# Loading batch 1's keys and queries right behind batch 0's, ahead of all weights, into a buffer of the MLP's activations

## The chip, the cores and the metric

The kernel runs on one core of a Trainium2 chip. The metric is device time in microseconds (us), the median of several executions; lower is better. A profile is one execution; its span is some 2 us shorter than the time of the same execution. The granted clock is the share of TensorE's full clock that the profile records as allowed, 1.0 or 0.5 here. A load is issued when its engine starts it, and lands when its last data are in place.

## The reference

Two layers: attention over blocks that a Sinkhorn-normalized matrix mixes, then a Fourier mix and an MLP. Cut to what matters:

```python
B, H, S, D = 4, 8, 768, 64          # batch, heads, sequence, head size
P = sinkhorn(sort_net)              # 5 rounds, [B, H, 8, 8]
k_sorted = einsum('bhij,bhjcd->bhicd', P, k_blocks)   # 8 blocks of 96 rows
v_sorted = einsum('bhij,bhjcd->bhicd', P, v_blocks)
attn = softmax(q_blocks @ k_sorted.T / 8) @ v_sorted  # within each block
x = attn.reshape(B, S, 512)
u = x + real(fft(fft(x, axis=1), axis=2))
out = u + relu(layernorm(u) @ w_ch1) @ w_ch2          # 512 -> 2048 -> 512
```

## The kernel before

Five engines work from one static program: TensorE (PE), VectorE (DVE), ScalarE (ACT), GpSimd (POOL) and SyncE (SP). The order on each engine is fixed when the kernel is built. GpSimd issues the loads that convert float32 to float16: k, q, v and the two weights. They share one queue, q0. SyncE issues the loads of constant tables, on another queue, q1.

K and q of a batch come in two halves of four heads. Each half has a tile of its own, from a pool of two buffers per name:

```python
    def load_qk(b, hf):
        for src, nm in ((k, "k"), (q, "q")):
            t = wt([128, 4, 6, D], F16, nm + "16", 2)      # two buffers
            start(nc.gpsimd.dma_start(t..., src[b, 4 * hf:4 * hf + 4, :, :]...))
            qk[nm, b, hf] = t

    load_qk(0, 0)
    # ... (cut)
    vst = wt([128, BLK, D], F16, "hr", 2, "vst")            # v of batches 0 and 1
    for g in range(2):
        start(nc.gpsimd.dma_start(vst[:, 48 * g:48 * g + 48, :], ...))
    load_qk(0, 1)
    # ... memsets; the Sinkhorn rounds, ph[9] is their last step (cut)
    # SyncE's tables: eb, vsf, tab, dtab, cs, and
    lt2 = const.tile([97, 2, S], F16, name="lt2")
    start(nc.sync.dma_start(lt2, cn["lt"].ap()))            # 97 rows
    # ...
    for c in range(4):
        w = nc.gpsimd.dma_start(w1sb[:, c, :], w1v[:, c, :])
        gated(w, ph[9]) if c == 0 else start(w)             # w1, after Sinkhorn
    # ... scores of batch 0 (cut)
    load_qk(1, 0)                                           # batch 1, first half
    # ... v_mix(0, n): the mixed v of batches 0 and 1 (cut)
    for c in range(2):
        start(nc.gpsimd.dma_start(w2sb[:, 4 * c:4 * c + 4, :], ...))
    load_qk(1, 1)                                           # batch 1, second half
    for c in range(2, 4):
        start(nc.gpsimd.dma_start(w2sb[:, 4 * c:4 * c + 4, :], ...))
    # v1_gen, later: load_v(1), v of batches 2 and 3, into vcx in two loads
```

The copy `q_copy(b, hp)` puts q in the order in which PE transposes it. It runs on VectorE (L281). VectorE also turns probabilities into the operand of the product with v (L421), and that product is PE's L444. In `mlp`, each group takes a tile of the pool "hr", which has two buffers. The tile `vst` takes the first one at the start; the second is unused until the MLP's second group.

The softmax here doesn't subtract the row's maximum and nothing guards it: scores larger than these inputs give would overflow.

Of the kernel before, what the change touches and what calls it, by code (L numbers as in the profile page):

```python
# [10 lines left out]
F16 = mybir.dt.float16  # L11
# [9 lines left out]
D = 64  # L21
# [79 lines left out]
def kernel(  # L101
# [10 lines left out]
    nc = tc.nc  # L112
# [19 lines left out]
    def wt(shape, dtype, tag, bufs, nm=None):  # L132
        cnt[0] += 1
        return work.tile(shape, dtype, tag=tag, bufs=bufs,
                         name=f"{nm or tag}{cnt[0]}")
# [36 lines left out]
    def start(ins):  # L172
        return tc.keep_in_program_order(ins)
# [5 lines left out]
    def traced():  # L179
        return list(nc.cur_bb.bb.instructions)  # L180
# [8 lines left out]
    qk = {}  # L189

    def load_qk(b, hf):
        for src, nm in ((k, "k"), (q, "q")):
            t = wt([128, 4, 6, D], F16, nm + "16", 2)
            start(nc.gpsimd.dma_start(
                t.rearrange("p h r d -> p h (r d)"),
                src[b, 4 * hf:4 * hf + 4, :, :].rearrange(
                    "h (p r) d -> p h (r d)", r=6)))
            qk[nm, b, hf] = t

    load_qk(0, 0)  # L200
    pack = const.tile([128, 240], F32, name="pack")
    start(nc.sync.dma_start(pack, cn["pack"].ap()))
# [34 lines left out]
    for n in range(NKS):  # L237
        t = const.tile([128, NB, 128], F16, name=f"ksb{n}")
# [12 lines left out]
    mone = const.tile([128, 3], F32, name="mone")  # L251
    start(nc.gpsimd.memset(mone, 1.0))
    start(nc.gpsimd.tensor_tensor(mone, mone, mhalf, op=ALU.pow))

    sec0 = len(traced())
    rmax = const.tile([32, NB], F32, name="rmax")
# [43 lines left out]
    w2sb = const.tile([128, 16, DM], F16, name="w2sb")  # L300
    w1v = moe_w_ch1.rearrange("(c p) f -> p c f", p=128)
    w2v = moe_w_ch2.rearrange("(c p) m -> p c m", p=128)
# [48 lines left out]
    t = wt([128, H, NB, 16], F16, "bdk", 2)  # L351
# [564 lines left out]
    def sc(kk):  # L916
        es = new_es()
        t0 = scores(*kk[:2], 0, es)
        t1 = scores(*kk[:2], 1, es)
        return kk + (es, [max(a, c) for a, c in zip(t0, t1)])  # L920
# [11 lines left out]
    nc.scalar.copy(tkh, psk)  # L932
    vb_make(0, psm)
    k0[1] = sc(k0[1])
    load_qk(1, 0)
    for n in range(16):
        v_mix(0, n)
    last = {}
    for ins in traced()[sec0:]:
        if ins.engine in (EN.DVE, EN.Activation, EN.PE):  # L940
            if ins.engine in last:
                dep(ins, last[ins.engine])
            last[ins.engine] = ins
    for c in range(2):
        start(nc.gpsimd.dma_start(w2sb[:, 4 * c:4 * c + 4, :],
                                  w2v[:, 4 * c:4 * c + 4, :]))
    load_qk(1, 1)
    for c in range(2, 4):
        start(nc.gpsimd.dma_start(w2sb[:, 4 * c:4 * c + 4, :],
                                  w2v[:, 4 * c:4 * c + 4, :]))  # L950
    add(0, fft_gen())
# [47 lines left out]
```

## Time and profile before

| | before |
|---|---|
| time, median of 3 | 323.6 us (322.8 to 323.98) |
| span of the profiled execution | 321.6 us |
| PE busy | 290.4 us, 90% |
| PE busy from 40 to 50, from 50 to 60 us | 6.06, 4.80 of 10 us |
| granted TensorE clock | 0.5 from 22.5 to 29.3 and from 49.8 to 63.4 us |

From the page of the kernel before, its second part: the span in 40 slices of 8 us, the busy share in tenths, and the granted clock.

```profile
PE   0389974699899999999999999999999999999995
...
PEclk9986995599999999999999999999999999999999
```

After the ninth slice (about 72 us) PE is nearly full to the end. What can be won is in the first slices. The seventh one and its neighbours show a dip, and the clock drops behind it. The table of stretches of the kernel before (us; busy time and count of each engine; granted clock; share of the DMA engines; GB/s) says the same:

```profile
40.00:50.00 10.00, 6.06 (x112) 4.83 (x111) 6.45 (x17) 6.85 (x15) 4.08 (x5) 0.99 0.86 140
50.00:60.00 10.00, 4.80 (x48) 3.62 (x48) 8.45 (x18) 1.17 (x3) 1.14 (x1) 0.50 1.40 201
```

The waits of PE in the kernel before (who waited for whom: us in total, times, longest):

```profile
PE pf L444 <- DVE eb L421: 4.5, 1, 4.5
PE pf L666 <- DVE ee L641: 3.6, 1, 3.6
```

PE waits for VectorE's L421. VectorE's own timeline tells why L421 is late (start, duration, what; in brackets the idle time before it and what ended it):

```profile
45.90 1.01 DVE L456 TENSOR_TENSOR r<-pf,rz 128x384 f16<-128x384 f32 x2
50.87 0.36 DVE L281 COPY qr<-q 128x768 f16<-128x768 f16 x1 [3.96 <-DMA q<-in_q_dram]
51.15 1.28 DVE L421 TENSOR_SCALAR eb<-ex 96x384 f16<-96x384 f32 x2
```

L421 has its inputs since 47 us, but stands behind the copy of batch 1's q. The copy waits for a load. The chain of waits of the kernel before, in order of time (start, duration, what), goes through that load:

```profile
21.34 0.74 POOL k L194
22.08 28.77 DMA q<-in_q_dram
50.85 0.02 issue
50.87 0.36 DVE qr L281
51.23 0.28 DVE eb L421
51.51 0.05 issue
51.56 1.15 PE pf L444 x12
```

So a load of 384 KB took 28.77 us from issue to landing. A chain says what came last, not what it would have cost to come earlier: of the 28.77 us, 3.96 show as a wait.

### The profile page before, as it was taken

To read this page: it belongs to the slowest core of one execution; us is meant where nothing else is said; L and a number is where in the kernel's file an instruction comes from. 1 tells how busy PE (TensorE), PEld (TensorE's weight loads), DVE (VectorE), ACT (ScalarE), POOL (GpSimd) and SP (SyncE) were. 2 spreads that over 40 slices of the span, in tenths; PEclk is the share of its full clock that TensorE was granted. 3 is DMA by queue.
4 is the path that set the end of the run, shared out by engine and by line. 5 is a ranking of instruction groups with operands and counts; after the bars stand their busy time and mean duration, and the time that the engine had idled before them with its cause. 6 is when DMAs were issued, how large, how long until landed. Compare 5 with 4: busy or idle time off the path is not lost.

```text
span 321.6 us, 5938 instructions
## 1 busy us (share of the span) xinstructions
PE 290.4 (90%) x2444; PEld 181.8 (57%) x2444; DVE 203.0 (63%) x454; ACT 122.6 (38%) x254; POOL 40.1 (12%) x73
## 2 busy tenths in 40 slices
PE   0389974699899999999999999999999999999995
PEld 0169853466777776455455656554664564554642
DVE  6795686888795656466495667644943662872831
ACT  2266481568789963012048843210460120110000
POOL 8320051013122010010003000100020010010000
PEclk9986995599999999999999999999999999999999
DMA  8999979971506070102111100021021120121002
GB/s 126 209 290 219 207 122 208 175 103 19 91 3 98 2 100 15 65 34 51 62 48 35 19 33 35 33 51 65 33 51 59 41 51 33 66 48 68 33 2 98
DMA packets 30131, 24.90 MB, mean 77 GB/s; under 512 B 15028, under 2 KB 25780, under 8 KB 30102
## 3 DMA queue, kind: packets, MB, share of 16 engines
q0 software_dynamic: 15552, 13.63, 27.3%
q1 hardware_dynamic: 14552, 10.89, 11.2%
q8 instruction: 19, 0.31, 0.4%
q14 instruction: 8, 0.07, 0.1%
HBM read 29.10 MB, written 6.29 MB: 110 GB/s over the span
## 4 chain that ended last, share of the span: by engine, by line
PE 70%; DMA 9%; ACT 9%; DVE 6%; issue 3%; POOL 2%; POOLq 0%; ACTq 0%
PE pm L802 26%; PE pm L785 24%; DMA q<-in_q_dram 9%; PE pf L749 7%; PE pf L444 4%; ACT ex L408 2%; PE pf L666 2%; PE pf L752 2%; PE pf L400 2%; ACT eb L424 1%; PE pf L375 1%; PE pf L386 1%; ACT vsf L167 1%; ACT un L714 1%; DVE eb L234 1%
## 5 line engine op out<-in xcount | busy, mean ns | idle before, releaser
L785 PE MATMUL pm<-ut,w1sb 128*128 128x384 f16 x512 | 92.5, 327 | 0.0
L802 PE MATMUL pm<-w2sb,hr 128*128 128x512 f16 x384 | 86.8, 379 | 0.0
L785 PEld LDWEIGHTS <-w1sb 128*128 128x128 f16 x512 | 49.8, 100 | 32.9 <-issue 1.2
L802 PEld LDWEIGHTS <-hr 128*128 128x128 f16 x384 | 37.3, 99 | 42.7
L794 ACT ACTIVATE hr<-pm 128x384 f16<-128x384 f32 x47 | 22.9, 493 | 99.1 <-PE pm L785 99.0
L790 DVE TENSOR_SCALAR hr<-pm 128x384 f16<-128x384 f32 x81 | 44.8, 555 | 20.7 <-PE pm L785 17.1
L811 DVE TENSOR_TENSOR u<-pm,u 128x512 f32<-128x512 f32 x24 | 16.5, 687 | 40.9 <-PE pm L802 40.9
L408 ACT ACTIVATE ex<-pf 96x384 f32<-96x384 f32 x64 | 28.2, 489 | 11.8 <-PE pf L400 11.6
L444 PE MATMUL pf<-vsf,eb 97*128 97x96 f16 x384 | 21.3, 211 | 5.5 <-DVE eb L421 4.5
L714 ACT ACTIVATE un<-u,nm,ny 128x512 f16<-128x512 f32 x20 | 15.6, 809 | 25.3 <-POOL nm L702 19.5
L698 POOL TENSOR_SCALAR mv<-mv 128x3 f32<-128x3 f32 x8 | 3.3, 417 | 173.5 <-DVE mv L760 173.5
L444 PEld LDWEIGHTS <-eb 97*128 97x128 f16 x384 | 19.5, 100 | 8.3 <-DVE eb L421 4.6
L424 ACT ACTIVATE eb<-ex,negone 96x384 f16<-96x384 f32 x38 | 23.1, 622 | 0.3
L495 PE MATMUL pm<-bdv,vcx 128*128 128x128 f16 x128 | 21.9, 267 | 1.0 <-DMA vcx<-k_dtab 0.5
L756 DVE SCALAR_TENSOR_TENSOR u<-r,pf 128x512 f32<-128x512 f16 x24 | 16.3, 681 | 9.5 <-DMA out_dram<-u 5.7
L497 PE MATMUL pm<-bdv,vbn 128*128 128x128 f16 x128 | 21.6, 237 | 0.0
L495 PEld LDWEIGHTS <-vcx 128*128 128x128 f16 x128 | 20.1, 173 | 1.3 <-issue 0.9
L497 PEld LDWEIGHTS <-vbn 128*128 128x128 f16 x128 | 17.4, 136 | 0.7 <-issue 0.7
L456 DVE TENSOR_TENSOR r<-pf,rz 128x384 f16<-128x384 f32 x32 | 17.1, 551 | 0.5
L759 DVE BATCH_NORM_STATS2 st<-u 128x6 f32<-128x512 f32 x24 | 16.5, 688 | 0.3
L167 ACT CAST vsf<-pm 96x512 f16<-96x512 f32 x18 | 14.3, 813 | 4.3 <-PE pm L497 4.0
L269 PE MATMUL pm<-vst,pack 128*128 128x512 f16 x12 | 4.2, 501 | 12.2 <-DMA vst<-in_v_dram 12.2
(103 smaller groups left out, 327.5 us busy)
## 6 DMA issues: line engine op xcount, KB each, us to landing
out_dram<-u SPq DMA_DIRECT2D x24, 256.0 KB, 2.0
k<-in_k_dram POOLq DMA_DIRECT2D x8, 384.0 KB, 8.2
q<-in_q_dram POOLq DMA_DIRECT2D x8, 384.0 KB, 9.4
w1sb<-in_moe_w_ch_dram POOLq DMA_DIRECT2D x4, 512.0 KB, 19.6
w2sb<-in_moe_w_ch_dram POOLq DMA_DIRECT2D x4, 512.0 KB, 25.1
vst<-in_v_dram POOLq DMA_DIRECT2D x2, 768.0 KB, 10.7
vcx<-in_v_dram POOLq DMA_DIRECT2D x2, 768.0 KB, 22.7
cs<-k_cs SPq DMA_DIRECT2D x1, 579.0 KB, 13.0
```

Source lines behind the costliest of these rows:

```text
L167: nc.scalar.copy(dst, src)
L408: nc.scalar.activation(ex.rearrange("p j (c r) -> p j c r", r=6), pss[h2][0:96].rearrange("p j (r c) -> p j c r", c=16), AF.Exp, scale=SCALE)
L424: nc.scalar.activation(ed, src, AF.Identity, bias=negone[0:96])
L444: nc.tensor.matmul(po[:, 65 * T:65 * T + 96], e[:, S * g + 256 * tt + 128 * n: S * g + 256 * tt + 128 * n + 128], vsf[:, vi:vi + 96], star ...
L495: nc.tensor.matmul(ps[:, dd, :], vcx[:, :, d], bd, start=True, stop=False)
L497: nc.tensor.matmul(ps[:, dd, :], vbn[t][:, d:d + 1].broadcast_to([128, 128]), bd, start=False, stop=True)
L714: nc.scalar.activation(un, ul[tt], AF.Identity, scale=y[:, tt:tt + 1], bias=nm[:, tt:tt + 1])
L749: nc.tensor.matmul(ps[:, c % 2::2], lh, dtab[:, c, :], start=(c == 0), stop=False, skip_group_check=True)
L785: nc.tensor.matmul(ps, w1sb[:, c, 128 * fc:128 * fc + 128], ut[:, c, :], start=(c == 0), stop=(c == 3))
L790: nc.vector.tensor_scalar(hr[:, fc, :], ps, 0.0, None, op0=ALU.max)
L794: nc.scalar.activation(hr[:, fc, :], ps, AF.Relu)
L802: nc.tensor.matmul(ps, hr[:, fc, 128 * tt:128 * tt + 128], w2sb[:, fc, :], start=(fc == 0), stop=(fc == 15))
```

## The change

The intent is to have batch 1's k and q early. The four loads go into the unused buffer of "hr", so they need not wait for batch 0 to free the double buffer, and they are issued ahead of w1.

```diff
+    def load_next():
+        t = wt([128, 2, 2, 4, 6, D], F16, "hr", 2, "kq1")
+        for hf in range(2):
+            for n, (src, nm) in enumerate(((k, "k"), (q, "q"))):
+                start(nc.gpsimd.dma_start(
+                    t[:, hf, n].rearrange("p h r d -> p h (r d)"),
+                    src[1, 4 * hf:4 * hf + 4, :, :].rearrange(
+                        "h (p r) d -> p h (r d)", r=6)))
+                qk[nm, 1, hf] = t[:, hf, n]
 ...
     start(nc.gpsimd.tensor_tensor(mone, mone, mhalf, op=ALU.pow))
+    load_next()
 ...
-    load_qk(1, 0)
     for n in range(16):
         v_mix(0, n)
 ...
-    for c in range(2):
-        start(nc.gpsimd.dma_start(w2sb[:, 4 * c:4 * c + 4, :], ...))
-    load_qk(1, 1)
-    for c in range(2, 4):
+    for c in range(4):
         start(nc.gpsimd.dma_start(w2sb[:, 4 * c:4 * c + 4, :], ...))
```

More of the change, by code (lines that the diff above doesn't have):

```diff
@@ L943 @@
             last[ins.engine] = ins
-    for c in range(2):
-        start(nc.gpsimd.dma_start(w2sb[:, 4 * c:4 * c + 4, :],
-                                  w2v[:, 4 * c:4 * c + 4, :]))
-    load_qk(1, 1)
-    for c in range(2, 4):
+    for c in range(4):
         start(nc.gpsimd.dma_start(w2sb[:, 4 * c:4 * c + 4, :],
```

## The prediction

> **What bounds the kernel now.** The page of the profile gives PE 90% busy in a span of 321.6 us, and the table of stretches shows PE busy 9.3 us or more in nearly every 10 us from 60 us on. From there the kernel is a full PE queue, with attention, the Fourier part and the MLP filling each other's gaps. Before 60 us it is not: PE is busy 6.06 us of 40 to 50 and 4.80 us of 50 to 60. The chain of waits names the cause: 28.77 us of "DMA q<-in_q_dram", from 22.08 to 50.85 us, 8.9% of the span. That is the query half that batch 1 needs first. Most of it is hidden; what shows is in the waits: VectorE's copy L281 of q waits 4.0 us for it (idle 46.91 to 50.87 in its timeline). The shift L421 of batch 0's last probabilities stands behind that copy in VectorE's order, so PE's L444 waits 4.49 us.
>
> The DMA is late because it is issued only at 21.3 us, when a matmul frees the double buffer, behind four loads of w1 (15 to 24 us each to landing). The next w2 and k/q loads queue behind it.
>
> **What changes.** No computation is added or removed. Comparing the instruction order of the two builds, PE, VectorE, ScalarE and SyncE have the same instructions in the same order; only the queue of GpSimd's DMAs is reordered. The four loads of batch 1's k and q (384 KB each) go out at about 8.7 us, where GpSimd idled from 8.7 to 13.5. Four issues at 0.76 us end near 11.8, before w1's gate at 13.2. The Sinkhorn steps took 1.77 us each whether GpSimd was issuing or idle, so I expect no slowdown there.
>
> **Will they be there in time?** Batch 0's second halves land at 19.1 and 25.1 us, as before. An undisturbed k or q load needs 1.9 us of the queue (82.5 to 84.5 us), but between 39 and 51 us one took 5.3. [...] Estimate at 5.3 us each: batch 1's first half by about 36 us, its second by 46. Needed: q at 46.9, second k at about 63. Enough slack. w1, w2 and v's second half shift: w1 lands near 50 instead of 39.4 us, and is first used at 85; w2 near 60, used at 124; v's at 70 or earlier, used at 76. None becomes a wait.
>
> **What it is worth.** 4.0 us of VectorE's wait, all on the chain, plus 0.2 us of small waits. Nothing after it is bound to a fixed time, so it carries to the end. The next wait (PE 3.6 us for L641, behind VectorE's chain of about 5 us from that copy to L636) stays and may grow to about 4.3. So the drop of the granted clock to 0.5, from 49.8 to 63.4 us, probably shortens or moves and does not vanish[...]. I count it as 0, within 1.5 us.
>
> **Prediction: 319.4 us, 8 in 10 between 317.6 and 321.3.** Faster by over 2%: 6%; within 2%: 93%; slower: 1%.
>
> **Right if:** no wait of L281 on a DMA; L444's wait under 0.8 us; L666 at about 55 us instead of 59.1; PE busy 9 us of 40 to 50; the DMA step gone from the chain.
>
> **Wrong if:** batch 1's loads still land after 47 us; the clock stays low longer in work that PE bounds (less gain); the clock never drops (up to 2 us more); the buffer shared with the MLP makes the second group's activations wait.

323.6 us less 4.0 for VectorE's wait and 0.2 for small waits is 319.4, with the clock counted as 0. That the early loads would take 5.3 us each, and that the drop of the clock goes with PE's wait, were estimates from the trace of before.

## The result, and the profile after

The changed kernel took 320.33 us (319.65 to 320.52, 4 runs) against 323.52 us (322.8 to 323.98, 4 runs). The ratio is 0.9897, with a 95% interval of 0.988 to 0.9914. A ratio is the mean time of one kernel's fast runs over that of the other's of the same rounds, so it is not quite the ratio of the medians. The gain is 3.3 us (0.0103 of 323.5).

In the changed kernel's line numbers 11 more lines stand ahead: L292 is before's L281, L432 is L421, L455 is L444, L652 is L641 and L677 is L666. The two rows of the page after, then two of its stretches:

```profile
PE   0399983998999999999999999999999999999995
...
PEclk9996998699999999999999999999999999999998
```

```profile
40.00:50.00 10.00, 8.31 (x151) 6.77 (x152) 8.00 (x23) 6.86 (x15) 2.70 (x3) 1.00 1.19 200
50.00:60.00 10.00, 5.66 (x64) 3.82 (x64) 9.07 (x19) 4.03 (x10) 2.63 (x3) 0.70 1.49 196
```

The waits of PE after:

```profile
PE pf L677 <- DVE ee L652: 4.3, 1, 4.3
PE pf L455 <- ACT ut L167: 0.9, 1, 0.9
PE pf L455 <- DVE eb L432: 0.7, 1, 0.7
```

PE's wait of 4.5 us has shrunk to 0.7, and the following wait grew from 3.6 to 4.3 us, as forecast. VectorE's timeline after has no wait for a load at the copy:

```profile
47.43 1.01 DVE L467 TENSOR_TENSOR r<-pf,rz 128x384 f16<-128x384 f32 x2
48.36 0.60 DVE L292 COPY qr<-kq 128x768 f16<-128x768 f16 x1
48.88 0.61 DVE L432 TENSOR_SCALAR eb<-ex 96x384 f16<-96x384 f32 x2
```

And the chain of waits after passes from the products through VectorE without a load:

```profile
47.51 0.93 DVE r L467 x2
48.44 0.52 DVE qr L292
48.96 0.53 DVE eb L432 x2
```

One number is odd. Taking 3.96 us of idle time out of VectorE should put the copy at 46.9 us; it stands at 48.36. Since both kernels have the same instructions in the same order on VectorE, the two traces can be laid over each other, instruction by instruction. The shift after minus before (each row read off the two timelines) is:

| work on VectorE, time in before | shift in the changed kernel |
|---|---|
| first operand of batch 0's k, 15.2 us | +0.2 us |
| L421, first, 19.4 us | +1.9 |
| mixing v, 26.8 us | +1.8 |
| mixing v, 29.9 us | +1.6 |
| the copy of q, 50.9 us | -2.5 |
| the next reciprocal, 52.4 us | -2.9 |
| from 66 us to the end | -3.1 |

So the changed kernel was late by about 1.5 us before it met the wait at all. In its trace the granted clock first rose to full at 19.9 us; in before's, at 15.7 us. The matmuls in between ran at half speed: those on v started 0.43 us apart, against 0.22 us in before. This needed a test of its own: is it the change's doing, or chance, and if it is chance, why is before's time as steady as the changed kernel's?

### The profile page after: what moved, and what is told of

The parts are those of the page before. It is cut to its first block, busy times and chain, and to the rows that moved or that the text cites. A ratio compares the mean times of both kernels' runs of the same rounds, so it can differ in the third digit from the quotient of the medians.

```text
span 318.5 us, 5938 instructions
## 1 busy us (share of the span) xinstructions
PE 290.7 (91%) x2444; PEld 181.4 (57%) x2444; DVE 202.4 (64%) x454; ACT 122.7 (39%) x254; POOL 40.2 (13%) x73
## 4 chain that ended last, share of the span: by engine, by line
PE 78%; ACT 9%; DVE 6%; DMA 3%; POOL 2%; issue 1%; POOLq 0%; ACTq 0%
PE pm L813 26%; PE pm L796 24%; PE pf L760 7%; PE pf L455 4%; DMA vst<-in_v_dram 3%; ACT ex L419 3%; PE pm L280 2%; PE pm L506 2%; PE pf L411 2%; PE pf L677 2%; PE pm L508 2%; PE pf L763 2%; ACT eb L435 2%; PE pf L397 1%; PE pf L386 1%
## 5 line engine op out<-in xcount | busy, mean ns | idle before, releaser
L813 PEld LDWEIGHTS <-hr 128*128 128x128 f16 x384 | 37.4, 99 | 42.7
L801 DVE TENSOR_SCALAR hr<-pm 128x384 f16<-128x384 f32 x81 | 44.8, 554 | 20.7 <-PE pm L796 17.1
L822 DVE TENSOR_TENSOR u<-pm,u 128x512 f32<-128x512 f32 x24 | 16.5, 686 | 41.0 <-PE pm L813 41.0
L725 ACT ACTIVATE un<-u,nm,ny 128x512 f16<-128x512 f32 x20 | 15.6, 809 | 25.2 <-POOL nm L713 19.4
L455 PE MATMUL pf<-vsf,eb 97*128 97x96 f16 x384 | 20.4, 206 | 1.7 <-ACT ut L167 0.9
L508 PE MATMUL pm<-bdv,vbn 128*128 128x128 f16 x128 | 21.3, 233 | 0.0
L455 PEld LDWEIGHTS <-eb 97*128 97x128 f16 x384 | 18.7, 98 | 4.4 <-issue 1.4
L770 DVE BATCH_NORM_STATS2 st<-u 128x6 f32<-128x512 f32 x24 | 16.5, 687 | 0.3
L280 PE MATMUL pm<-vst,pack 128*128 128x512 f16 x12 | 5.3, 614 | 12.4 <-DMA vst<-in_v_dram 12.4
L167 ACT CAST vsf<-pm 96x512 f16<-96x512 f32 x18 | 14.3, 813 | 3.6 <-PE pm L508 3.3
## 6 DMA issues: line engine op xcount, KB each, us to landing
w2sb<-in_moe_w_ch_dram POOLq DMA_DIRECT2D x4, 512.0 KB, 21.3
```

The lines of the kernel that those rows point to most:

```text
L455: nc.tensor.matmul(po[:, 65 * T:65 * T + 96], e[:, S * g + 256 * tt + 128 * n: S * g + 256 * tt + 128 * n + 128], vsf[:, vi:vi + 96], star ...
L508: nc.tensor.matmul(ps[:, dd, :], vbn[t][:, d:d + 1].broadcast_to([128, 128]), bd, start=False, stop=True)
L770: nc.vector.bn_stats(st, u)
L801: nc.vector.tensor_scalar(hr[:, fc, :], ps, 0.0, None, op0=ALU.max)
L813: nc.tensor.matmul(ps, hr[:, fc, 128 * tt:128 * tt + 128], w2sb[:, fc, :], start=(fc == 0), stop=(fc == 15))
```

## The experiments

The theory after the first reading, A: what counts is when the first q of batch 1 lands, and that is set by the bytes which stand ahead of it in the queue. Rivals: B, the late issue (the buffer is freed only at 21 us); C, something narrower in how the load is served; D, the gain comes from other loads which also moved (w2, v, batch 2). The twelve further runs, below the two traces read so far (r_after and r_before are the two kernels once more):

| kernel | clock first full (us) | first q lands | copy's wait for it | second v load lands | span | time: median, range, runs | ratio to before, 95% |
|---|---|---|---|---|---|---|---|
| before | 15.7 | 50.8 | 4.0 | 73.6 | 321.6 | 323.52 (322.8 to 323.98), 4 | 1 |
| changed | 19.9 | 38.1 | none | 73.6 | 318.5 | 320.33 (319.65 to 320.52), 4 | 0.9897 (0.988 to 0.9914) |
| behind_w1 | 19.7 | 51.7 | 3.3 | 73.9 | 322.5 | 323.71 (323.09 to 324.29), 6 | 1.0 (0.9986 to 1.0014) |
| order_only | 20.2 | 40.3 | none | 73.5 | 319.7 | 321.47 (321.29 to 324.75), 6 | 0.9955 (0.9924 to 0.9987) |
| half1_only | 21.0 | 55.9 | 6.8 | 74.5 | 326.7 | 328.12 (327.56 to 328.48), 4 | 1.0134 (1.012 to 1.0149) |
| lt96_before | 15.2 | 38.9 | none | 64.8 | 317.2 | 319.05 (318.87 to 319.26), 4 | 0.9854 (0.9839 to 0.9868) |
| r_after | 15.4 | 38.1 | none | 73.4 | 317.7 | 319.82 (319.53 to 320.6), 4 | 0.9884 (0.9867 to 0.9901) |
| lt96_after | 15.1 | 29.3 | none | 62.0 | 316.6 | 319.51 (318.38 to 321.04), 6 | 0.9886 (0.9864 to 0.9908) |
| half0_only | 20.7 | 37.4 | none | 73.4 | 319.5 | 321.34 (321.06 to 322.59), 6 | 0.9934 (0.9917 to 0.9952) |
| r_before | 20.7 | 51.0 | 2.3 | 73.7 | 322.2 | 324.15, 1 | - |
| warm_before | 6.1 | 51.3 | 2.9 | 73.6 | 322.2 | 323.69 (323.05 to 324.22), 6 | 0.9993 (0.9977 to 1.0009) |
| warm_after | 8.6 | 37.7 | none | 73.2 | 317.5 | 320.11 (319.35 to 321.08), 5 | 0.9885 (0.9866 to 0.9904) |
| warm_v_after | 8.9 | 37.9 | none | 63.1 | 314.8 | 318.34 (316.62 to 320.71), 6 | 0.984 (0.9808 to 0.9872) |
| warm_lt96 | 6.0 | 39.0 | none | 65.7 | 318.1 | 318.66 (318.43 to 320.81), 6 | 0.9858 (0.9833 to 0.9882) |

Times and ratios are those of all timed runs of a kernel; the other columns come from the one execution that was profiled, so the rise of its clock need not be that of the other executions. All of these kernels gave correct results. In each, PE, VectorE and ScalarE have the same instructions in the same order as before, but for the dummy matmuls of the last four. The median of before in the three later series was 323.7 to 323.8 us (11 runs each).

### 1. The new buffer without the place in front: behind_w1

```diff
-    load_next()                 # ahead of w1
     for c in range(4):
         w = nc.gpsimd.dma_start(w1sb[:, c, :], w1v[:, c, :])
         gated(w, ph[9]) if c == 0 else start(w)
+    load_next()                 # behind w1
```

> The four early loads keep the MLP's buffer, so nothing of batch 0 has to free it, but they are issued right behind the four w1 loads instead of ahead of them. Theory A (place in the queue: the bytes in front of q decide): batch 1's first q still lands near 50 us, VectorE's L281 copy still waits about 4 us, ratio to before 0.998 to 1.002. Rival B (the late issue at 21.3 us, when a matmul frees the double buffer, is what makes q late): q lands by 45 us, no wait, ratio about 0.990 like the change.

The first q was issued at 16.5 us instead of 22.1, and yet landed at 51.7. The waits of VectorE in this kernel:

```profile
DVE qr L291 <- DMA kq<-in_q_dram: 3.3, 1, 3.3
```

The time is that of before. The buffer, and with it the earlier issue, is worth nothing by itself. Rival B falls, and with it one half of the cause that the prediction gave.

### 2. The place in front without the new buffer: order_only

```diff
     load_qk(1, 0)               # old double buffer, issued when batch 0 frees it
+    for c in range(4):          # w1 moved here, behind it
+        w = nc.gpsimd.dma_start(w1sb[:, c, :], w1v[:, c, :])
+        gated(w, ph[9]) if c == 0 else start(w)
     for n in range(16):
         v_mix(0, n)
```

> No new buffer: batch 1's first k and q keep the double buffer and are still issued at about 21.3 us, but w1's four loads are issued behind them. Theory A (place in the queue): first q lands near 38 us as in the change, no wait of the copy, ratio 0.988 to 0.992. Rival B (buffer and late issue): q as late as before or only a few us earlier, ratio above 0.996.

The first k and q were issued at 23.5 and 24.3 us, later than in before. Q landed at 40.3 us, 10.5 us earlier than in before. The first wait is gone. The ratio, 0.9955, misses the expected band: only about 1.5 us were won. VectorE's waits show one reason:

```profile
DVE qr L281 <- DMA q<-in_q_dram: 1.4, 1, 1.4
```

This is the copy of the *second* half of q. It was not moved in this kernel and landed at 60.3 us. The work around it now runs earlier, so that load has become a wait. It was absorbed in this trace, where the clock rose late (20.2 us): the shift against before is -2.1 us at the first copy, -0.5 at the copy that needs the second half and -2.0 from 66 us on. Four of the six runs lie within 321.29 and 321.61 us; the other two, 323.32 and 324.75 us, are about as slow as before, and without a trace of them the reason stays open.

### 3. The wrong half in front: half1_only

```diff
-        for hf in range(2):
+        for hf in (1,):         # in load_next, ahead of w1
 ...
+    load_qk(1, 0)               # first half: back behind w1, double buffer
```

> Only the second half of batch 1's k and q goes ahead of w1; the first half, which is needed first, stays behind w1 in the double buffer. Theory (the landing of the first q sets the time one for one): 768 KB more stand in front of it, at 1.9 us of the queue each, so it lands near 54.7 us instead of 50.9, the copy waits about 8 us instead of 4, and the kernel is slower than before by about 3.9 us (ratio near 1.012). Rival (the gain of the change comes from something else that also moves, such as earlier w2, v or batch 2 loads): a gain of part of the 3.2 us, or nothing.

The first q landed at 55.9 us, and VectorE's waits have:

```profile
DVE qr L292 <- DMA q<-in_q_dram: 6.8, 1, 6.8
```

The span grew by 5.1 us (326.7 against 321.6) for a q that landed 5.1 us later (55.9 against 50.8), and the ratio, 1.0134, means 4.3 us. The wait is 6.8 us and not the 8 expected, since the work ahead of it was 2.2 us later than in before's trace (the clock rose at 21.0 us). W2, v and batch 2 moved here as well, and nothing was gained. In this trace the landing of the first q sets the time one for one. Rival D falls as an explanation of the first 3 to 4 us.

### 4. Nothing moved, one row fewer: lt96_before

Why did that load take 28.77 us when an undisturbed one takes 1.9 us of the queue? In the packets of before's trace, 960 of the 1,024 packets of the first k and q (768 bytes each) had started by 37.3 us. The other 64 started only later. 64 is exactly one sixteenth. In the same time the table `lt` was moved: 97 packets of 3,072 bytes, one after another, from 23 to 49 us, at no moment two of them under way; of w1's 512 packets, which started between 20.4 and 38.6 us, up to 19 were under way at once. The author guessed that the row count of 97 makes the table go that way, and that its slow passage holds back the load. Row 96 of the table is written by the kernel itself before it is read, so it need not be loaded:

```diff
-    start(nc.sync.dma_start(lt2, cn["lt"].ap()))
+    start(nc.sync.dma_start(lt2[0:96], cn["lt"].ap()[0:96]))
```

> The kernel before with one edit: the table lt is loaded in 96 rows instead of 97 (row 96 is written by the kernel itself before it is read). In the trace of before the 97 rows are 97 packets of 3,072 bytes one after the other from 23 to 49 us, and of batch 1's first k and q 960 of 1,024 packets had started by 37.3 us, while the last 64 started between 39 and 51. Theory C [...] q lands at 37 to 40 us with its issue and place unchanged, no wait of the copy, ratio 0.988 to 0.992, the same gain as the change. Rival A alone (bytes ahead in the queue decide): q lands at 48 us or later, ratio above 0.995.

The issues of batch 1's first k and q, before (KB each, us from issue to landing):

```profile
k<-in_k_dram POOLq DMA_DIRECT2D x1, 384.0 KB, 24.2
q<-in_q_dram POOLq DMA_DIRECT2D x1, 384.0 KB, 28.8
```

The same issues in lt96_before:

```profile
k<-in_k_dram POOLq DMA_DIRECT2D x1, 384.0 KB, 15.3
q<-in_q_dram POOLq DMA_DIRECT2D x1, 384.0 KB, 16.5
```

The issue of `lt` itself, from another window of each trace: first before, where the view has no time to landing for it, then lt96_before, where it lands 12 us after its issue (the last of before's 97 rows starts at 49.0 us, 34 us after the issue at 15.2):

```profile
lt<-k_lt SPq DMA_DIRECT2D x1, 291.0 KB
...
lt<-k_lt SPq DMA_DIRECT2D x1, 288.0 KB, 12.0
```

With nothing moved in GpSimd's queue, q landed at 38.9 us, the wait vanished, and the ratio is 0.9854, more than the change itself and more than the 0.988 to 0.992 expected (v lands 9 us earlier here as well, which section 5 comes to). So theory A was right about the place only as far as it went. What held q back was not mainly the bytes of w1 ahead of it: behind the same w1, with 96 rows instead of 97 in a table of another queue, it lands 12 us earlier. How the table's rows hold back the last sixteenth of the load is not shown, since the trace does not say which engine moved a packet. What before's trace shows are times. From 24.7 to 38.9 us there are 32 gaps of about 300 ns between one packet of `lt` and the next, while w1's packets, 324 ns each, were moved. Of the later gaps 52 are about 55 ns long; from 39.2 to 44.6 us one packet of k or q, 79 ns each, starts every 0.19 us, as does one of `lt`.

The change puts q ahead of w1; its q lands 12.7 us earlier than before's. It does not touch the table: in the changed kernel's trace the 97 rows still go one after another, from 23.4 to 41.4 us.

### 5. Where the missing microsecond went: r_after and r_before

Both are the kernels unedited, for a second trace.

> The changed kernel again, unedited, to see how much of the gap between 4.2 us forecast and 3.2 us measured is the TensorE clock of the first 30 us. In the trace of after the granted clock rose first at 19.9 us, in that of before at 15.7, and the work from 17 to 47 us ran 1.5 us later. Theory P (phase: before hides such a delay in its wait for q, after can't): this run's span follows its first rise, near 318.5 us if the rise is at 19 us or later, near 317.0 if it is before 16; time before minus this 3.0 to 4.8 us. Rival (the early loads themselves slow the first 47 us): the 1.5 us delay is there whatever the clock does.

> The kernel before again, unedited, for one more trace of its first 52 us. Theory P: q lands at 50 to 52 us whatever the clock does, so if the first rise comes at 19 us or later, the work up to 47 us is later by about 1.5 us and the wait of L281 is shorter by the same (2.5 us instead of 4.0), with the time unchanged at 323 to 324 us. Rival: the wait stays 4.0 us and the time grows by 1.5.

In r_after the clock rose at 15.4 us, in r_before at 20.7. So both kernels see an early and a late rise, and theory P holds for the first 47 us. In r_before the work up to 47 us was later by 2.0 us, and the wait for q was shorter by about as much:

```profile
DVE qr L281 <- DMA q<-in_q_dram: 2.3, 1, 2.3
```

Q landed at 51.0 us all the same, and the span is 322.2 against 321.6 us. The wait takes up what the clock costs. This is why before is steady. In the changed kernel there is no such wait: in r_after, with the early rise, the copy is 4.2 us earlier than in before and the next reciprocal 4.9 us (before's pair of L421 took 1.28 us while GpSimd issued a load of v beside it, here it took 0.62). After the first rise the recorded clock changed at 22.49, 29.31, 49.79 and 63.45 us in before, and at 23.27, 30.10, 53.99 and 60.82 us in the changed kernel. The ten traces without dummy matmuls fall into two groups by the first rise: four at 15.1 to 15.7 us, six at 19.7 to 21.0, none between. What decides between the two is not shown.

But r_after did not reach 317.0 us of span, as expected of an early rise; it came to 317.7. The shift against before is -4.9 us until 76 us (before's time) and -3.9 us from 78 us on. PE's waits in r_after from 60 to 80 us name what is new:

```profile
PE pf L455 <- ACT ut L167: 0.9, 1, 0.9
PE pm L280 <- DMA vcx<-in_v_dram: 0.8, 1, 0.8
```

The second load of v for batches 2 and 3 lands at 73.4 us in r_after, as in before (73.6): it is the last of the same bytes in the same busy queue. PE's matmuls on it begin at 76.1 us in before, but at 71.2 in r_after. A load that had slack has become the next floor, the load whose landing now sets when PE can go on. The prediction had v at "70 or earlier" and ruled such a wait out.

### 6. Only the half that is needed first: half0_only

```diff
-        for hf in range(2):
+        for hf in (0,):         # in load_next, ahead of w1
 ...
     for c in range(2): ...      # w2
+    load_qk(1, 1)               # second half: where it was
     for c in range(2, 4): ...   # w2
```

> Only the first half of batch 1's k and q goes ahead of w1, into the MLP's buffer; the second half stays where it was. Theory (only the first q is on the chain): q lands near 38 us, no wait of the copy, ratio 0.985 to 0.991, all of the change's gain. Rival (the second half or the later w2 and v matter too): half of the gain, ratio 0.994 to 0.996.

The ratio is 0.9934, about 2.1 us and not 3.3: the expectation of all of the gain was missed, and the rival's is nearer. The second q landed at 60.2 us:

```profile
DVE qr L292 <- DMA q<-in_q_dram: 1.7, 1, 1.7
```

As in order_only, this trace's clock rose late, its wait was absorbed by 66 us, and the final shift (-2.2 us) is the one at the first copy. Five of the six runs of half0_only and four of the six of order_only lie between 321.06 and 322.11 us, and none of either is below. That fits a second floor at 60 us which the full change moves out of the way (its second q lands at 44.6 us). That the times rest on this floor in the runs without a trace is inferred.

### 7. Both: lt96_after

The edit of lt96_before, on top of the change.

> The changed kernel with the table lt loaded in 96 rows. If the change and the 96 rows both work only by bringing the first q in before 46.9 us, they do not add up: same time as the better of the two alone, ratio to before 0.985 to 0.991. If the changed order or the early w2, v and batch 2 loads have a worth of their own, the two add to about 8 us, ratio near 0.976.

The two do not add up: 0.9886, against 0.9854 and 0.9884 to 0.9897 alone. The change has no worth of its own besides bringing the loads in. In its trace (early rise) v landed at 62.0 us, PE's wait for it is gone, and the shift stays at -5.1 us to the end, where r_after fell back to -3.9. But its six runs spread from 318.38 to 321.04 us, and their mean is no better than r_after's.

### 8. The clock taken out of the game, and v moved: the four warm kernels

At the start PE waits for v, in before until 12.2 us. Ninety dummy matmuls were put there, where they start at about 3.3 us, to bring the clock up before the first real one:

```diff
+    warm = pm([128, 128])
+    for n in range(90):
+        start(nc.tensor.matmul(warm, idh, idh))
```

warm_before, warm_after and warm_lt96 are before, the change and lt96_before with these lines. warm_v_after also moves v ahead of w2:

```diff
+    load_v(1)                   # was issued after w2, by v1_gen
     for c in range(4):
         start(nc.gpsimd.dma_start(w2sb[:, 4 * c:4 * c + 4, :], ...))
```

> The kernel before with 90 dummy matmuls (128 x 128 x 128, on the identity, result unused) put in front of PE's first work, in the 9 us in which PE waits for v. They should raise the granted clock before 12.4 us in every run, so that the first real matmuls run at full clock and the work up to 47 us comes 1.2 us or more earlier than in the trace of before. Theory (before hides its early stage in its wait for q, which lands near 51 us): the wait of L281 grows to 4.5 us or more and the time stays, ratio 0.998 to 1.002. Rival (the early clock counts in both kernels alike): ratio 0.992 to 0.996.

> The changed kernel with the same 90 dummy matmuls. Theory (with q early, the early stage counts, until v of batches 2 and 3 lands at 73.4 us and becomes the floor): faster than the changed kernel's 320.0 us, but not below 319 us, because PE's L280 on vcx now waits for v 1.5 us or more; ratio to before 0.984 to 0.988. Without that floor it would reach about 317.7 us, ratio 0.982.

> As warm_after, and v's two loads for batches 2 and 3 are issued ahead of w2's four instead of behind them. Theory (v is the floor of the changed kernel): v lands near 64 us, the wait of L280 on it is gone, and the kernel is 1 to 2 us faster than warm_after: 316.7 to 318.2 us, ratio 0.978 to 0.984. Rival (no floor by v): the same time as warm_after.

> The order of the kernel before (no early loads), with lt in 96 rows and the same 90 dummy matmuls. In lt96_before q landed at 38.9 us and v at 64.8, so neither is a floor here. If the two floors (q, v) and the early clock are all there is, this runs like warm_v_after, 316.7 to 318.2 us, ratio 0.978 to 0.984, without the change.

The dummies failed at what they were for. They brought the clock up at 6.0 to 8.9 us, but in warm_before and warm_lt96 it fell again at 13.0 and 12.8 us and came back only at 19.8 and 19.6. In warm_after and warm_v_after it held until 22.3 and 22.5 us. In the two traces in which it fell, PE's wait for v was 2.9 and 2.4 us long; in the two in which it held, the longest was 2.0 and 1.2 us. No limit follows: in before it fell at 22.5 us, and PE's longest wait from 15.7 to 22.5 us was 0.8 us. So they didn't take chance out, and the times don't test the early clock cleanly. Warm_before kept before's time (0.9993), as expected, but its wait was 2.9 us, not 4.5: its clock was late, not early. It is one more case of the wait taking up a delay (the work ahead of it was 1.5 us later than before's). The gain forecast for warm_after did not come: 0.9885, the same as r_after.

The comparison within the four still speaks about v. In warm_after the second v landed at 73.2 us and PE waited for it, 0.4 us in this trace. In warm_v_after it landed at 63.1 us and the wait is gone. The mean of all runs is 320.09 us for warm_after and 318.64 us for warm_v_after, 1.45 us less, in the range that was expected; the two intervals (0.9866 to 0.9904 and 0.9808 to 0.9872) overlap by a hair. In the trace of warm_v_after the shift against before is -6.8 us and stays so to the end. Warm_lt96, which reaches both early landings without the change, has 0.9858, short of the 0.978 to 0.984 expected; its interval, 0.9833 to 0.9882, overlaps that of warm_v_after.

The lowest medians are thus those of warm_v_after (318.34 us), warm_lt96 (318.66 us) and lt96_before (319.05 us, with one edited line and the narrowest range); their intervals overlap, so the runs do not rank them. All three lie below the changed kernel's medians of 319.82 and 320.33 us.

## Why the prediction was right, point by point

- **What bounds the kernel before: right.** The copy's wait for batch 1's first q, 4.0 us, was on the chain. Half1_only shows it one for one in the other direction: 5.1 us later, 5.1 us of span.
- **Why q was late: half wrong.** "Issued only at 21.3 us, when a matmul frees the double buffer" is not the cause: an issue at 16.5 us changed nothing (behind_w1), and one at 24.3 us was early enough (order_only). "Behind four loads of w1" is true, but hides the cause: the table of 97 rows. With 96 rows, q lands at 38.9 us behind the same w1. That the change worked all the same is partly luck: a place ahead of w1 helps on either account of the delay.
- **When the moved loads land: right.** 38.1 us for the first q (36 forecast) and 44.6 us for the second (46 forecast). The sum came right by luck in part: 5.3 us for each of the four loads were assumed, and they landed 6.2, 6.1, 4.6 and 1.9 us apart.
- **W1, w2 and v: partly wrong.** W1 landed at 55.3 us (about 50 forecast) and w2 at 65.5 (about 60), both far ahead of their use. V landed at 73.6 us, not at 70 or earlier. The bytes in the queue are the same and v is last, so it lands when it did before.
- **"Nothing after it is bound to a fixed time, so it carries to the end": the step that failed.** With an early clock 4.9 us were won at 52 us and 1.0 of them were given back at about 73 us, where PE then waits for v (r_after's time). With a late clock the start costs 1.5 to 2.0 us, which before hides in its wait and the changed kernel can't.
- **The size.** 4.2 us were forecast; 3.3 us (ratio 0.9897) and 3.8 us (0.9884 of 323.7) were measured. The term for the removed wait was right. What was missing are two terms of up to 1 and up to 2 us which replace each other: with a late clock v is no floor, with an early one it is.
- **The next wait and the clock: right.** L641's wait for PE grew to 4.3 us, and the time at half clock around 50 to 60 us fell from 13.7 to 6.8 us.
- **Signs in the profile.** No DMA wait of the copy: yes. L444's wait under 0.8 us: yes, 0.7 for VectorE (its 0.9 for ScalarE's L167 was there before, too). L666 at about 55 us: 55.96. PE busy 9 us of 40 to 50: no, 8.31. The late start is not the reason: r_after, with the early rise, has 8.23.

What stays open: why the clock first rises at 15.1 to 15.7 us in four traces and at 19.7 to 21.0 in six, though PE's first matmuls start at 12.2 us in before (early) and 12.4 in the changed kernel (late); how the table's rows hold back a load of another queue; what lengthened the two q copies in the changed kernel's trace (0.60 and 0.68 us beside GpSimd's issues of v; 0.35 and 0.39 us in r_after, where the first ran ahead of the issues and the second met only the end of one), where only the coincidence in time is shown; why the four runs of lt96_before lie so close together (0.4 us) while those of lt96_after spread over 2.7 us, with one trace of each; and how warm_v_after's gain splits between v's place and the dummies, since v's place was not run without them.

## What to carry to other kernels

When a load lands late, look at which of its packets start last, and at what else is moved then, before moving the load: 15 sixteenths of the packets of the first k and q had started by 37.3 us, and loading 96 rows of an unrelated table instead of 97 won 4.7 us, more than rearranging the queue. A wait for a transfer is also a cushion: it hides delays ahead of it, and once it is removed, these delays and the next transfer in the queue (here q's second half at 60 us, then v at 73 us) take over, so list the landing times of all later loads and compare each with its use after the shift. Two executions of one kernel differed by 4.5 us (the changed kernel) and 5.1 us (before) in when the TensorE clock first rose, which moved the work behind it by 1.7 and 1.9 us; lay two traces over each other before explaining a difference of that size by the edit.
